# Attention, routed experts and a dense layer in one kernel: the last stage in parts of 512, 512, 512 and 256 tokens, and routing's end spread over three engines

## The chip, the cores and the metric

The kernel runs on one core of one Trainium2 chip. The metric is device time in microseconds; the median of three runs is given with the lowest and the highest. The profiles come from the hardware profiler, one execution each.

## The reference

Three steps follow one another on 4 x 448 = 1792 tokens of width 768. The kernel's output is the last step's, in float32.

```python
# attention, 4 batches, 12 heads, 448 tokens, head width 64; a sigmoid in place of a softmax
scores = q @ k.T / sqrt(64) - log(448)
x = sigmoid(scores) @ v                    # heads side by side: 1792 x 768
# experts: each token goes to one of 8, chosen by the cosine with the expert's vector
logits = normalized(x) @ normalized(expert_emb).T / tau
e = argmax(logits);  gate = softmax(logits)[e]
x = gate * (relu(x @ w1[e]) @ w2[e])       # 768 -> 1024 -> 768
# a dense layer with a rational activation, 768 -> 2048 -> 768
h = x @ w_in
P = a0 + a1*h + a2*h*h + a3*h**3;  Q = 1 + |b0|*|h| + |b1|*h*h
out = (P / (Q + 1e-6)) @ w_out
```

## The kernel before

All products that need float32 accuracy are made from a high and a low part of each operand (`fp32r`): three products on TensorE for one of the reference.

**Attention** (`attention`) runs in twelve turns `T` of two pairs of heads each, three turns a batch. A turn puts on TensorE's queue, in this order: scores, values of the turn before, scores, the transpositions of the finished heads (`transp`), the scores and values of the last 64 keys. ScalarE makes the sigmoids, VectorE copies the transposed rows out of PSUM (L241) and does side work. A batch's **routing** is a generator, `route_steps`. It is put in a queue at the end of the turn in which the batch's rows are complete; each later turn takes eight steps of it (L466), behind the turn's own instructions. Its steps on VectorE reduce the logits (L263), find the maximum and the one-hot table `OH`, copy that as bf16 to `OHb` (L282), and sum it per batch in `OHs` (L284, L287). Then come the rank products `rk` on TensorE (L295 to L305) from `OHb` and the previous batches' `OHs`, and on VectorE the rank's row and tile and the four masks `AC` (L331). The last batch is the tail: its steps are emitted without a break after the last turn and interleaved with `plan`.

**Plan** counts the tokens of each expert (`cn`, L542), makes the first tile of each expert (`bp`, copied to `bs` at L556 by VectorE), and from the masks the row list `IDX` (L580) of 21 slots of 128 rows. GpSimd gathers a slot's rows with `IDX` (L698).

**Experts** (`experts`): `x_hi` transposes a slot's rows on TensorE (L712) and casts them, `x_lo` makes the low part by two subtracting products (L718), `mm` are the expert products (L775), and the results go out by an indirect DMA on GpSimd's queue (L844). `either(s)` loads a flag on TensorE, ScalarE and GpSimd and branches between a slot with at most 64 rows in use and a full one. The first thing in a slot's `ahead` is the gather of the slot after next. VectorE turns the weights of expert after expert into high and low parts (L663, L670); before it writes a weight it waits until the last slot of the expert before has used the old one. `gates` makes the gate values, 112 tokens a line.

**The last stage** (`ffn`) goes through the tokens in `NQ` = 4 parts of 448. Each part runs over 16 blocks of 128 hidden units, 64 units in all. A unit is 18 products into `ph` (`l1`, L985 to L989), an activation of six operations on ScalarE and eight on VectorE (`act1`, `act2`), and 18 products into `acc` (`l2`, L1028 to L1030), which are emitted two units later. In the first part each block's weights are loaded, split and stored to DRAM (`load`, `split`, `keep`); the later parts fetch the split weights back (`fetch`), 2 x 768 KB a unit, two units ahead in SP's queue. The next part's rows are loaded (`rows`), gated on VectorE (`gate`, L949) and transposed on TensorE in pieces of 112 tokens (`xprep`, L958). For the first part `first_x` does that, behind 26 products of ones (L969).

Order on each engine is the order in which the instructions are written; semaphores are set by the framework.

## Time and profile before

| | |
|---|---|
| median of 3 runs | 1050.55 us (1050.28 to 1054.69) |
| the profiled execution: its time | 1050.22 us |
| its span | 1048.4 us |
| TensorE busy | 1007.6 us, 96% of the span |
| VectorE, ScalarE, GpSimd busy | 726.4, 506.0 and 136.9 us |
| granted clock of TensorE, mean | 0.987 |
| chain of waits, by engine | PE 87%, DVE 6%, DVE's queue 2%, DMA 2% |

PE is TensorE's products, PEld its weight loads, DVE is VectorE, ACT ScalarE, POOL GpSimd, SP the queue that issues most transfers. L12 is line 12 of the kernel before. Attention lasts to about 180 us, the experts to about 551 us, the last stage to the end. "Idle before" names the instruction that ended an engine's wait. In the rows the merged pieces of an engine carry a count (x12).

### The profile page before, as it was taken

What the parts mean: (1) busy time and instruction counts of PE and PEld (TensorE: products, weight loads), DVE (VectorE), ACT (ScalarE), POOL (GpSimd) and SP (SyncE); (2) the same over time, 40 slices, a digit from 0 to 9 for tenths busy, and PEclk for the clock granted to TensorE, in tenths of its full rate; (3) what the DMA queues carried; (4) which work ended last, traced back from release to release, by engine and by line L of the source; (5) the groups of instructions that cost most, each with busy time, mean ns of one, the idle gap of its engine ahead of it and who ended that gap; (6) DMA issues with size and microseconds to landing.
All of it is one profiled execution on the core that took longest, in us unless ns stands there. A gap on an engine that the chain in (4) does not pass through costs nothing.

```text
span 1048.4 us, 14336 instructions
## 1 busy us (share of the span) xinstructions
PE 1007.6 (96%) x5239; PEld 832.6 (79%) x5240; DVE 726.4 (69%) x1038; ACT 506.0 (48%) x859; POOL 136.9 (13%) x139
## 2 busy tenths in 40 slices
PE   8999998579999999999988999999999999999998
PEld 3444444468998998889876989999999999999997
DVE  1645565899607896496975999867676677666765
ACT  5556665532332323333335767655554645464453
POOL 2000000243223333243440000000000000000000
PEclk9999999699999999999998999999999999999999
DMA  7987875686906869367878996759664876548631
GB/s 216 280 229 227 256 238 182 218 269 208 360 32 206 272 204 345 104 232 272 288 261 299 381 369 269 301 189 373 208 208 151 310 290 204 205 160 327 220 128 53
DMA packets 103051, 250.19 MB, mean 239 GB/s; under 512 B 8296, under 2 KB 61928, under 8 KB 102960
## 3 DMA queue, kind: packets, MB, share of 16 engines
q1 hardware_dynamic: 99888, 234.39, 65.5%
q0 software_dynamic: 3072, 14.58, 3.9%
q8 instruction: 58, 0.95, 0.4%
q14 instruction: 33, 0.27, 0.1%
HBM read 193.88 MB, written 55.05 MB: 237 GB/s over the span
## 4 chain that ended last, share of the span: by engine, by line
PE 87%; DVE 6%; DVEq 2%; DMA 2%; issue 1%; SPq 1%; ACT 0%; POOL 0%; POOLq 0%; ACTq 0%
PE ph L775 11%; PE py L775 11%; PE ph L985 8%; PE ph L986 7%; PE acc L1028 7%; PE ph L989 7%; PE acc L1029 7%; PE acc L1030 7%; PE po L221 5%; PE sc L181 5%; DVEq L672 2%; PE po L240 2%; PE pt L712 2%; DVE w2l L670 1%; PE sc L194 1%
## 5 line engine op out<-in xcount | busy, mean ns | idle before, releaser
L985 PE MATMUL ph<-xh,wi 128*128 128x448 f32 x384 | 142.6, 371 | 0.0
L986 PE MATMUL ph<-xh,wi 128*128 128x448 f32 x384 | 140.9, 367 | 0.0
L1028 PE MATMUL acc<-gh,wo 128*128 128x448 f32 x384 | 140.5, 366 | 0.0
L1030 PE MATMUL acc<-gl,wo 128*128 128x448 f32 x384 | 140.5, 366 | 0.0
L1029 PE MATMUL acc<-gh,wo 128*128 128x448 f32 x384 | 140.5, 366 | 0.0
L994 ACT COPY h<-ph 128x448 f32<-128x448 f32 x64 | 34.0, 532 | 165.3 <-PE ph L989 164.0
L1001 DVE SCALAR_TENSOR_TENSOR sq<-sq,ab,ab 128x448 f32<-128x448 f32 x64 | 43.7, 683 | 98.4 <-ACT ab L998 98.4
L989 PE MATMUL ph<-xl,wi 128*128 128x448 f32 x384 | 88.6, 366 | 0.0
L986 PEld LDWEIGHTS ph<-xh,wi 128*128 128x128 f32 x384 | 72.6, 189 | 5.8
L985 PEld LDWEIGHTS ph<-xh,wi 128*128 128x128 f32 x384 | 72.6, 189 | 5.8
L989 PEld LDWEIGHTS ph<-xl,wi 128*128 128x128 f32 x384 | 72.1, 188 | 6.1
L1028 PEld LDWEIGHTS acc<-gh,wo 128*128 128x128 f32 x384 | 72.1, 188 | 6.1
L1030 PEld LDWEIGHTS acc<-gl,wo 128*128 128x128 f32 x384 | 72.1, 188 | 6.1
L1029 PEld LDWEIGHTS acc<-gh,wo 128*128 128x128 f32 x384 | 72.1, 188 | 6.0
L185 ACT ACTIVATE A<-sc,bias_s 128x896 f32<-128x896 f32 x72 | 67.2, 1004 | 11.2 <-PE sc L181 11.1
L663 DVE CAST w0h<-raw 128x1536 fp32r<-128x1536 f32 x14 | 12.8, 957 | 79.1 <-ACTq L788 78.2
L775 PE MATMUL py<-w2h,h 128*128 128x384 f32 x256 | 62.8, 344 | 4.3 <-DVEq L672 3.9
L775 PE MATMUL ph<-w0h,x 128*128 128x512 f32 x192 | 59.5, 410 | 7.8 <-DVEq L672 3.7
L785 ACT ACTIVATE hs<-ph 128x512 f32<-128x512 f32 x38 | 22.7, 599 | 81.5 <-PE ph L775 81.5
L775 PE MATMUL py<-w3h,h 128*128 128x384 f32 x256 | 61.3, 339 | 0.0
L181 PE MATMUL sc<-qr,kr 64*128 64x448 f32 x288 | 60.6, 553 | 0.0
L775 PE MATMUL ph<-w1h,x 128*128 128x512 f32 x192 | 60.5, 403 | 0.0
(203 smaller groups left out, 2012.0 us busy)
## 6 DMA issues: line engine op xcount, KB each, us to landing
raw<-in_w_dram SPq DMA_DIRECT2D x64, 768.0 KB
wi<-ws SPq DMA_DIRECT2D x48, 768.0 KB
wo<-ws SPq DMA_DIRECT2D x48, 768.0 KB
raw<-in_w_in_dram SPq DMA_DIRECT2D x16, 768.0 KB
raw<-in_w_out_dram SPq DMA_DIRECT2D x16, 768.0 KB
wd<-dec SPq DMA_DIRECT2D x32, 384.0 KB
rw<-wd SPq DMA_DIRECT2D x16, 768.0 KB
ws<-wi SPq DMA_DIRECT2D x16, 768.0 KB
```

What stands on the lines that cost most here:

```text
L181: nc.tensor.matmul(sc[:, r, :S], lhsT=d["k"][rs, c * P : (c + 1) * P], rhs=d["q"][rs], start=True, stop=True)
L185: nc.scalar.activation(A, sc[:, :, :S], AF.Sigmoid, bias=st["bias_s"], scale=0.125)
L221: nc.tensor.matmul(po[r * D : r * D + D, :S], lhsT=vts[pi // 3 % 2][:, c, 2 * (pi % 3) + r], rhs=d["A"][c][:, r], start=False, stop=(c == 2),)
L775: m = nc.tensor.matmul(d[u], lhsT=a, rhs=w, start=(g == 0 and n == 0), stop=(g == 1 and n == len(work) - 1))
L985: nc.tensor.matmul(ph, lhsT=w[:, 0, js], rhs=xh[:, k], start=(k == 0), stop=False)
L986: nc.tensor.matmul(ph, lhsT=w[:, 1, js], rhs=xh[:, k], start=False, stop=False)
L989: nc.tensor.matmul(ph, lhsT=w[:, 0, js], rhs=xl[:, k], start=False, stop=(k == KD - 1))
L994: nc.scalar.copy(h, ph)
L1001: nc.vector.scalar_tensor_tensor(sq, sq, ab1, ab, op0=ALU.mult, op1=ALU.add)
L1028: nc.tensor.matmul(a, lhsT=w[:, 0, js], rhs=gh, start=(f == 0), stop=False)
L1029: nc.tensor.matmul(a, lhsT=w[:, 1, js], rhs=gh, start=False, stop=False)
L1030: nc.tensor.matmul(a, lhsT=w[:, 0, js], rhs=gl, start=False, stop=(f == NF - 1))
```

## The change

- The last stage's parts are 512, 512, 512 and 256 tokens. Rows are handled in pieces of 128 tokens instead of 112. So the gate values are turned to 128 a line by two transfers through DRAM, `gd` and `gr`, on SP's queue behind the last expert's weights.
- The fetch of kept weights is written three units ahead instead of two.
- A turn of attention takes eleven routing steps instead of eight. There is one more empty step ahead of the rank products.
- In the tail the sum of the last batch's one-hot table is left out; `cn` is made by four products from `OHb` and one from the earlier sum. Two of four masks `AC` go from VectorE to GpSimd, the copy `bs` from VectorE to ScalarE. The temporaries of `plan` lie in the constants' pool.
- At the end of `plan` 16 products of ones (128 x 128 by 128 x 512, bf16) are put on TensorE; four more stand between the first slot's `x_hi` and `x_lo`, and four behind `x_lo`.
- The gather of the slot after next moves from `ahead` into the slot, behind `x_lo` of the next slot.

The diff, cut; the places left out give the activation's tiles the part's width and drop the unused pool.

```diff
--- before.py
+++ after.py
@@ -40,6 +40,8 @@
 EARLY = ((0, 0), (0, 1), (1, 0), (1, 1), (2, 0), (3, 0), (2, 1), (3, 1))
+WARM = 16
+OT = 6
 THR = 3.4332275390625e-05
...
@@ -280,13 +281,15 @@
             nc.vector.tensor_copy(ohb, oh)
-            s4 = ap.tile([P, NE], F32, name="s4")[:CP]
-            nc.vector.tensor_reduce(s4, oh.rearrange("p c e -> p e c"), axis=AX.X, op=ALU.add)
-            yield
-            if b:
-                nc.vector.tensor_add(OHs[:CP, b], s4, OHs[:CP, b - 1])
-            else:
-                nc.vector.tensor_copy(OHs[:CP, b], s4)
+            if not tail:
+                s4 = ap.tile([P, NE], F32, name="s4")[:CP]
+                nc.vector.tensor_reduce(s4, oh.rearrange("p c e -> p e c"), axis=AX.X, op=ALU.add)
+                yield
+                if b:
+                    nc.vector.tensor_add(OHs[:CP, b], s4, OHs[:CP, b - 1])
+                else:
+                    nc.vector.tensor_copy(OHs[:CP, b], s4)
+            yield
             yield
@@ -328,7 +331,7 @@
                 ci = b * NCB + c
-                nc.vector.tensor_scalar(
+                (nc.gpsimd if tail and c > 1 else nc.vector).tensor_scalar(
                     AC[:CP, ci],
@@ -463,7 +466,7 @@
                 values3(T)
-            for _ in range(8):
+            for _ in range(11):
                 if queue and next(queue[0], 1) == 1:
@@ -482,7 +485,7 @@
         norm_some(len(norms))
-        steps = plan(tc, st, pl, psc)
+        steps = plan(tc, st, cst, psc)
         for g in queue:
@@ -539,7 +542,9 @@
     cn = ps.tile([NE, 1], F32, name="cn", tag="sc")
-    nc.tensor.matmul(cn, lhsT=st["OHs"][:CP, B - 1], rhs=st["ones"][:CP, :1], start=True, stop=True)
+    for c in range(NCB):
+        nc.tensor.matmul(cn, lhsT=st["OHb"][:CP, NCH - NCB + c], rhs=st["ones"][:CP, :1], start=(c == 0), stop=False)
+    nc.tensor.matmul(cn, lhsT=st["OHs"][:CP, B - 2], rhs=st["ones"][:CP, :1], start=False, stop=True)
     yield
@@ -553,7 +558,7 @@
     bs = pl.tile([P, 2 * NE], F32, name="bs")
-    nc.vector.tensor_copy(bs, bp)
+    nc.scalar.copy(bs, bp)
     tm = pl.tile([P, NCH, NE], F32, name="tm")[:CP]
@@ -602,6 +607,9 @@
     nc.vector.tensor_copy(FL[0:1], es)
+    wp = ps.tile([P, 2, 512], F32, name="wp", tag="sc")
+    for _ in range(WARM):
+        nc.tensor.matmul(wp[:, 0], lhsT=st["ones"], rhs=st["wz"], start=True, stop=True)
 
@@ -701,6 +709,11 @@
             )
+
+        def ones(n):
+            wp = pph.tile([P, 512], F32, name="ph")
+            for _ in range(n):
+                nc.tensor.matmul(wp, lhsT=st["ones"], rhs=st["wz"], start=True, stop=True)
 
@@ -808,7 +821,6 @@
                 xg_alloc(s + 2)
-                gather(s + 2)
             if s + 1 < NSLOT:
@@ -834,6 +846,8 @@
                 x_lo(s + 1)
+            if s + 2 < NSLOT:
+                gather(s + 2)
             mm(s, 3, 0)
@@ -868,7 +882,9 @@
         x_hi(0)
+        ones(4)
         x_lo(0)
+        ones(4)
         for i in range(4):
@@ -878,6 +894,10 @@
         flush()
+        gd = drm.tile([NT], F32, name="gd")
+        st["gr"] = cst.tile([P, NT // P], F32, name="gr")
+        nc.sync.dma_start(gd.rearrange("(c p) -> p c", p=CP), st["gt"][:CP])
+        nc.sync.dma_start(st["gr"], gd.rearrange("(c p) -> p c", p=P))
         either(0)
@@ -892,10 +912,11 @@
     wd, yd, ident = st["wd"], st["yd"], st["ident"]
-    gt = st["gt"]
+    gt = st["gr"]
     co, ab1, one = st["co"], st["ab1"], st["one"]
     NF = F2 // P
-    NQ = B
+    Q = [(t, min(512, NT - t)) for t in range(0, NT, 512)]
+    NQ = len(Q)
     NU = NQ * NF
@@ -915,7 +936,7 @@
         def fetch(i):
-            if NF <= i < NU:
+            if NF <= i < NU and i not in WI:
                 pair(i)
@@ -936,50 +957,48 @@
         def rows(q, parts):
-            yq = fp.tile([P, NCB, DM], F32, name="yq", bufs=1)
-            src = yd[q * S : (q + 1) * S].rearrange("(c p) d -> p c d", p=CP)
-            n = NCB // parts
-            for c in range(0, NCB, n):
-                nc.sync.dma_start(yq[:CP, c : c + n], src[:, c : c + n])
-            X[q] = dict(y=yq)
+            t0, w = Q[q]
+            yq = fp.tile([P, 4, DM], F32, name="yq", bufs=1)
+            src = yd[t0 : t0 + w].rearrange("(c p) d -> p c d", p=P)
+            n = w // P // parts
+            for c in range(0, w // P, n):
+                nc.sync.dma_start(yq[:, c : c + n], src[:, c : c + n])
+            X[q] = dict(y=yq, n=w, c=w // P)
 
         def gate(q, c):
-            ci = q * NCB + c
-            y = X[q]["y"][:CP, c]
-            nc.vector.tensor_scalar(y, y, gt[:CP, ci : ci + 1], None, op0=ALU.mult)
+            if c >= X[q]["c"]:
+                return
+            ci = Q[q][0] // P + c
+            y = X[q]["y"][:, c]
+            nc.vector.tensor_scalar(y, y, gt[:, ci : ci + 1], None, op0=ALU.mult)
 
...
             if k == 0:
-                d["h"] = fw.tile([P, KD, S], F32R, name="xh")
-                d["l"] = fw.tile([P, KD, S], F32R, name="xl")
-            pt = pph.tile([P, 512], F32, name="ph")
-            for c in range(NCB):
-                nc.tensor.transpose(
-                    pt[:, c * CP : (c + 1) * CP], d["y"][:CP, c, k * P : (k + 1) * P], ident[:CP, :CP]
-                )
-            nc.scalar.copy(d["h"][:, k], pt[:, :S])
-            nc.vector.tensor_sub(d["l"][:, k], pt[:, :S], d["h"][:, k])
+                d["h"], d["l"] = [fw.tile([P, KD, 512], F32R, name=n)[:, :, : d["n"]] for n in ("xh", "xl")]
+            pt = pph.tile([P, 512], F32, name="ph")[:, : d["n"]]
+            for c in range(d["c"]):
+                nc.tensor.transpose(pt[:, c * P : (c + 1) * P], d["y"][:, c, k * P : (k + 1) * P], ident)
+            nc.scalar.copy(d["h"][:, k], pt)
+            nc.vector.tensor_sub(d["l"][:, k], pt, d["h"][:, k])
 
...
             d = X[0]
-            d["h"], d["l"] = [fw.tile([P, KD, S], F32R, name=n) for n in ("xh", "xl")]
+            d["h"], d["l"] = [fw.tile([P, KD, 512], F32R, name=n) for n in ("xh", "xl")]
             pts = [ppa.tile([P, 512], F32, name=f"acc{k}") for k in range(KD)]
...
                 nc.tensor.matmul(pts[0], lhsT=st["ones"], rhs=st["wz"], start=True, stop=True)
-            for c in range(NCB):
+            for c in range(4):
                 for k in range(KD):
-                    nc.tensor.transpose(
-                        pts[k][:, c * CP : (c + 1) * CP], d["y"][:CP, c, k * P : (k + 1) * P], ident[:CP, :CP]
-                    )
+                    nc.tensor.transpose(pts[k][:, c * P : (c + 1) * P], d["y"][:, c, k * P : (k + 1) * P], ident)
             for k in range(KD):
-                nc.scalar.copy(d["h"][:, k], pts[k][:, :S])
-                nc.vector.tensor_sub(d["l"][:, k], pts[k][:, :S], d["h"][:, k])
+                nc.scalar.copy(d["h"][:, k], pts[k])
+                nc.vector.tensor_sub(d["l"][:, k], pts[k], d["h"][:, k])
 
...
             xh, xl = X[i // NF]["h"], X[i // NF]["l"]
-            ph = pph.tile([P, 512], F32, name="ph")[:, :S]
+            ph = pph.tile([P, 512], F32, name="ph")[:, : X[i // NF]["n"]]
             for k in range(KD):
...
...
@@ -1019,32 +1042,33 @@
             w = WO.pop(i)
+            t0, m = Q[q]
             gh, gl = G.pop(i)
...
                     acc[o] = ppa.tile([P, 512], F32, name=f"acc{o}")
-                a = acc[o][:, :S]
+                a = acc[o][:, :m]
                 js = slice(o * P, (o + 1) * P)
...
                 if f == NF - 1:
-                    ot = fp.tile([P, S], F32, name="ot", bufs=6)
+                    ot = fp.tile([P, 512], F32, name="ot", bufs=OT)[:, :m]
                     if o % 2 and q == NQ - 1:
...
                         nc.scalar.copy(ot, a)
-                    nc.sync.dma_start(out[o * P : (o + 1) * P, q * S : (q + 1) * S], ot)
+                    nc.sync.dma_start(out[o * P : (o + 1) * P, t0 : t0 + m], ot)
 
...
         split(1)
-        rows(0, NCB)
+        rows(0, 4)
         keep(0)
...
         load(5)
-        for c in range(NCB):
+        for c in range(4):
             gate(0, c)
@@ -1053,7 +1077,7 @@
                         rows(q + 1, 1)
-                    if 5 <= f < 5 + NCB:
+                    if 5 <= f < 9:
                         gate(q + 1, f - 5)
@@ -1062,7 +1086,8 @@
                 fetch(i + 2)
-                act2(i, *act1(ph))
+                fetch(i + 3)
+                act2(i, *act1(ph, X[i // NF]["n"]))
             if i >= LF:
```

## Rows read from the trace of the kernel before

**Rows 1.** Windows by stage: busy us (instructions) of PE, PEld, DVE, ACT, POOL; clock; DMA.

```profile
20.00:180.00 160.00, 159.04 (x935) 74.76 (x935) 87.98 (x175) 95.56 (x125) 0.00 (x0) 1.00 0.79 241
...
203.00:253.00 50.00, 43.40 (x223) 37.16 (x222) 48.04 (x32) 17.08 (x38) 22.25 (x16) 0.97 0.80 262
...
565.00:685.00 120.00, 118.77 (x588) 108.41 (x587) 109.66 (x172) 81.62 (x137) 0.00 (x0) 0.99 0.88 340
```

**Rows 2.** Timeline, first and last of three batches: start us, us, engine, operation.

```profile
76.80 2.53 PE L181 MATMUL sc<-qr,kr 64*128 64x448 f32 x12
...
77.31 0.18 DVE L282 CAST OHb<-OH 112x32 bf16<-112x32 f32 x1
...
159.16 2.53 PE L181 MATMUL sc<-qr,kr 64*128 64x448 f32 x12
...
159.60 0.18 DVE L282 CAST OHb<-OH 112x32 bf16<-112x32 f32 x1
```

**Rows 3.** Timeline of routing's end for the last batch, VectorE and GpSimd.

```profile
180.68 0.60 DVE L331 TENSOR_SCALAR AC<-iof,PM,tok 112x128 f16<-112x128 f32 x2
...
185.23 1.11 DVE L331 TENSOR_SCALAR AC<-iof,PM,tok 112x128 f16<-112x128 f32 x4
...
188.50 0.18 DVE L580 TENSOR_SCALAR IDX<-ip 128x21 int32<-128x21 f32 x1 [0.25 <-PE ip L571]
...
189.55 1.11 POOL L698 DMA_INDIRECT xg<-xd,IDX  x1 [181.54 <-DVE EB L591]
```

**Rows 4.** Timeline from the gathered rows to VectorE's next weights.

```profile
193.67 1.51 PE L712 MATMUL pt<-ident,xg 128*128 128x128 f32 x6 [5.09 <-DMA xg<-xd,IDX]
...
197.99 0.77 PE L775 MATMUL ph<-w0h,x 128*128 128x512 f32 x1 [1.49 <-ACT x L719]
...
202.92 1.83 DVE L663 CAST w0h<-raw 128x1536 fp32r<-128x1536 f32 x2 [1.65 <-ACTq L788]
```

**Rows 5.** Timeline of the products of ones ahead of the last stage.

```profile
552.16 7.46 PE L969 MATMUL acc<-wz,ones 128*128 128x512 bf16 x25 [4.10 <-PEq L887]
```

**Rows 6.** Windows, the first expert products (columns as in rows 1).

```profile
198.00:201.80 3.80, 3.80 (x9) 3.03 (x10) 1.55 (x7) 2.41 (x5) 0.00 (x0) 0.50 1.03 378
```

**Rows 7.** Chain of waits, merged: start us, us, engine, tile, line, count.

```profile
257.92 6.27 PE ph L775 x27
...
270.56 6.25 PE py L775 x36
...
598.52 1.24 PE ph L989 x6
...
1024.65 1.22 PE ph L989 x6
...
1031.95 1.22 PE ph L989 x6
```

**Rows 8.** Timeline of SP's loads for the last stage and their first reader.

```profile
536.52 6.46 SPq L911 DMA_DIRECT2D rw<-wd  x3
...
551.99 0.83 ACT L930 CAST wi<-rw 128x768 fp32r<-128x768 f32 x1 [2.11 <-PEq L887]
```

**Rows 9.** Timeline of a row of products with 64 moving columns.

```profile
536.24 1.00 PE L743 MATMUL pt<-fold,hs 128*128 128x64 f32 x8
```

**Rows 10.** Waits: engine, tile, line, releaser: us in total, times, longest.

```profile
PE ph L958 <- DVE yq L949: 1.2, 1, 1.2
```

**Rows 11.** Chain of waits: the last stage's first rows.

```profile
556.42 6.18 DMA yq<-yd
```

**Rows 12.** Timeline of the last unit's activation and of the end.

```profile
1033.20 0.54 ACT L994 COPY h<-ph 128x448 f32<-128x448 f32 x1 [3.56 <-PE ph L989]
...
1039.59 0.62 DVE L1016 TENSOR_TENSOR gl<-t,gh 128x448 fp32r<-128x448 f32 x1
...
1044.14 0.62 DVE L1034 COPY ot<-acc 128x448 f32<-128x448 f32 x1 [0.59 <-PE acc L1030]
```

**Rows 13.** Windows, a stretch in which only the kept weights are fetched.

```profile
720.00:724.00 4.00, 4.00 (x21) 3.71 (x20) 2.40 (x5) 2.71 (x5) 0.00 (x0) 1.00 1.02 419
```

20 lines of the change are left out of this document (11 added, 9 removed).

## The prediction

> **What bounds the kernel now.** I read three views, in this order. First the busy time by stage [rows 1]: in attention TensorE is busy for 159.04 of 160 us, so any wait put in front of it there is paid in full. From 203 to 253 us it is VectorE that is full (48.04 of 50 us): it splits the weights of the first experts, and the experts' products wait for it. In the first part of the last stage TensorE is full again (118.77 of 120 us) with VectorE close behind (109.66). Second the timeline of the three places where TensorE stands still: between attention and experts, where the chain of routing, the gather and the first products follow one another; between experts and last stage; and after the last product. Third the chain of waits and the waits by name, for the price of a product and for what stops TensorE in the last stage. Their rows are named where they are used.
>
> The sum is made against the profiled execution, 1050.22 us with a span of 1048.4 us; it lies 0.3 us under the median of the three runs, 1050.55 us.
>
> **Eleven routing steps instead of eight.** A batch's routing is a generator of which TensorE's rank products are one step. With eight steps in a turn the rank products fall into the next turn, when VectorE's one-hot table is long done. With eleven they are the eleventh step of the same turn and stand in TensorE's queue right behind the values products, ahead of the next scores. TensorE reaches that place at 76.80 us, but the table in bf16 (L282) ends only at 77.31 + 0.18 = 77.49 us [rows 2]; with 0.05 us for the signal that is a wait of 0.74 us. Behind the waiting product all scores and values are queued, and TensorE has no slack here [rows 1]. There are three such batches, each with the same order; the last one gives 159.60 + 0.18 + 0.05 - 159.16 = 0.67 us [rows 2]. Sum 3 x 0.7 = **+2.1 us**; bounds 0 (TensorE late for another reason) and 2.4.
>
> **The chain of routing for the last batch.** The eleven steps take leftovers of batch 2, 0.60 us, out of the way (first row of [rows 3]). Two of four masks go to GpSimd: 0.56 of 1.11 us on VectorE (second row of [rows 3]). The count from four products of bf16 tables and one sum costs TensorE four products more and VectorE a reduction and an addition less; I take it at nothing. The copy of the bases on ScalarE saves VectorE one short copy; it goes into the margin, because GpSimd's two masks beside VectorE may cost as much. So the indices come 1.2 us earlier, at 188.50 - 1.2 = 187.3 us. From indices to first transposition the trace has 193.67 - 188.50 = 5.2 us [rows 3, 4], most of it the gather; its data would be there at 192.5 us.
>
> **The products of ones** are queued on TensorE between routing's last product (about 187.2 us) and the transpositions of the first rows. Their price is bounded from both sides: 25 of the same shape took 7.46 us, partly at half clock [rows 5], so 16 take 4.8 us at that pace; at half clock throughout nine products of 512 columns took 3.80 us [rows 6], so 16 take 6.8 us. I take 5.9 us: they end at 193.1 us (192.0 to 194.0), after the data, and eat most of what the shorter chain gains. The transpositions then start at 193.1 instead of 193.67 us. From there to the first expert product the trace has 197.99 - 193.67 = 4.3 us [rows 4]: transpositions, a cast, two subtracting products, and then some two microseconds in which TensorE's sequencer loads the slot's flags and branches. At full clock the first items are shorter, but two times four ones (0.86 us each at full clock) are queued among them, and the second four stand ahead of the flag's load. Net I take +0.6 us (0 to 0.9), so the first product starts at 198.0 us, as before. What is gained is the clock: the clock granted from 198.0 to 201.8 us was 0.50, the 1.2 GHz level [rows 6], and the slot's first twelve products ran until VectorE went on at 202.92 us [rows 4]. At full clock twelve cost 12 x 0.232 = 2.8 us [rows 7], so VectorE can go on at 201.0 us: **-1.9 us** (bounds -2.5, where VectorE's own gates are next, and +0.5, if the clock is low again). This counts in full, since VectorE is the bound up to 253 us.
>
> The transpositions of the first rows ran at the low clock and did not raise it [rows 4, 6]. The Trainium skill (TensorE: Matmul & The Clock Gate, section on PE-mode transpose) says that a transposition doesn't count as activity for the clock; by that rule the ones have to carry it alone, and the gap while the sequencer branches speaks against them. That is a rival below.
>
> **Moved transfers.** The gather of the rows after next moves from ahead of a slot to its middle, on GpSimd's queue behind the slot's subtractions. It needed 4.1 us to its use [rows 3, 4]; it has a slot's products left, over 27 x 0.232 + 36 x 0.174 = 12.5 us [rows 7]. Nothing, and GpSimd's subtractions come earlier, under VectorE's bound. The two transfers that turn the gate values from 112 to 128 lines go on SP's queue behind the last expert weights, ahead of the last stage's loads, and the second waits for the first to land. Behind them stand loads that were issued by 543 us and read first at 551.99 us [rows 8]. Elements of 4 bytes have no row here; as long as both together stay under 9 us they cost nothing, so I take 0 (0 to 2).
>
> **The last stage.** Its columns are the same, 3 x 512 + 256 = 4 x 448, and so are its 2304 products. The price follows the columns: 384 columns 6.25 / 36 = 0.1736 us, 448 columns 7.30 / 36 = 0.2028 us, 512 columns 6.27 / 27 = 0.2322 us [rows 7]; per column that is 0.452, 0.453, 0.4535 ns. At 0.4525 ns 256 columns cost 0.116 us. A floor by the weights' load shows where 64 moving columns still took (1.00 - 0.22) / 7 = 0.111 us from start to start, the last one's 0.22 us taken as its length [rows 9], under 0.116. Before: 2304 x 0.2028 = 467.3 us, and about 1 us more since the first part ran at 1.24 / 6 = 0.2067 us for its first seven units. After: 1728 x 0.2322 + 576 x 0.116 = 468.1 us. Taken at **-0.6 us**; bounds: 512 columns at the lower price per column and 256 at the floor give -4, 256 columns at 0.123 us and the first part slower in the same proportion give +6.
> TensorE's one pause, 1.2 us before a transposition that waited for VectorE's gating [rows 10], goes: a unit of 36 products lasts 8.36 us instead of 7.44 and VectorE's operations on 512 columns grow by about half a microsecond. **-1.2 us** (0 to -1.2). 72 transpositions of 112 columns become 60 of 128, 5% fewer columns: nothing. The first rows are 128 lines a transfer instead of 112, 14% more of the 6.18 us that they are waited for [rows 11]: **+0.5 us** (0 to 0.9).
> At the end the last unit's activation runs from 1033.20 to 1040.21 us while TensorE does two blocks of second products [rows 12]; it just fitted. With 256 columns the two blocks last 36 x 0.116 = 4.2 us. Scaled by columns the activation would take 4.0 us, unscaled 7.0; half of it fixed gives 5.4: a new wait of 1.2 us. The last copy (0.62 us, [rows 12]) and the stores shrink by some 0.4 us. **+0.8 us** (-0.4 to +2.4).
> A unit of the last part fetches 1.573 MB in 4.2 us, 375 GB/s; the same fetch ran at 419 GB/s [rows 13], so it keeps up. The Trainium skill (DMA: Bandwidth & Descriptors, Specifications) gives about 358 GB/s per core, by which the part would be short by 0.2 us a unit; the trace disagrees, and the measurement decides. Even at the 340 GB/s of the mixed stretch [rows 1] it would miss 16 x 0.43 = 7 us, less than the three units (12.6 us) by which the buffers lead.
>
> **Sum:** 2.1 - 1.9 - 0.6 - 1.2 + 0.5 + 0.8 = -0.3 us, so 1050.22 - 0.3 = **1049.9 us**.
>
> **Rivals.** (a) The gains come and the waits don't: routing's wait is covered (0 instead of +2.1), the products take their lower prices (-3.5), the end fits (0). Sum -1.9 - 3.5 - 1.2 + 0.5 = -6.1: 1044 us. For it: the price per column of the shorter products is the lower one. Against it: the order of the queue in [rows 2] leaves no cover. (b) Slower: a product of 256 columns doesn't get below the time that loading and handing over its weights takes. Each nanosecond over 0.116 us costs 576 x 0.001 = 0.58 us; from 0.127 us on the whole is over 0.5% slower, at 0.13 us it is 1058 us. For it: a weights record lasts about 0.19 us, more than the product. Against it: [rows 9]. (c) The change doesn't do what it says: the clock is low again at the first product, so the ones only delay; +0.5 instead of -1.9 gives 1052 us. (d) The last part waits for its fetches: only below 315 GB/s (16 x 0.79 us a unit use up the lead); at 290 GB/s 16 x 1.2 - 12.6 = 7 us more, 1057 us. Against it: [rows 13].
>
> **How the numbers follow.** Forecast 0.60, (a) 0.20, (b) 0.09, (c) 0.09, (d) 0.02. A measurement of this kernel can tell about 0.5%, 5.3 us, from no change. Case (a) is faster and the forecast reaches under 1045.3 us in a few cases; (b) and a rest of the forecast are slower: faster 0.22, same 0.66, slower 0.12. The forecast alone spans 1046 to 1054 us; the range takes in most of (a) and (c) and a part of (b): 1044.0 to 1055.5 us.
>
> **What would show it.** A wait of 0.7 us on TensorE before the rank products in three turns of attention; ones ending between 192 and 194 us plus that shift, with transpositions right behind; granted clock 1.00 at the first expert products; 0.232 and 0.116 us a product in the last stage; no pause before the transpositions; a wait of about 1.2 us before the last block. It is wrong above all if 256 columns cost more than 0.12 us, or if the rank products don't wait.

## The result

The changed kernel takes 1044.81 us (median of 8 runs, 1041.90 to 1047.02) against 1051.87 us of the kernel before on the same chip (8 runs, 1047.35 to 1054.69): ratio 0.9911, 95% interval 0.9881 to 0.9940. It is faster by 0.9%. No change was forecast as likeliest, at 1049.9 us; the time lies inside the range, near its lower end. The profiled execution of after took 1043.8 us with a span of 1042.0 us, 6.4 us under the 1048.4 us of before.

Cut into stretches at events that both traces have (end of the last product of attention, VectorE's last weights of its full stretch, at 253.3 and 254.7 us, end of the experts' products, first and last product of the last stage, end), the spans divide so, in us:

| stretch | before | after | difference |
|---|---|---|---|
| start to end of attention | 180.28 | 184.32 | +4.04 |
| to VectorE's last weights | 73.01 | 70.37 | -2.64 |
| to the end of the experts' products | 294.77 | 294.62 | -0.15 |
| hand-over, to the first product of the last stage | 17.16 | 18.95 | +1.79 |
| first to last product of the last stage | 478.52 | 469.27 | -9.25 |
| to the end | 4.67 | 4.50 | -0.17 |

The gain is in the last stage, where I had put -1.8 us. Everything else together costs 2.9 us. Of the 4.04 us in attention 2.2 us are the waits ahead of the rank products; the other 1.9 us lie ahead of 40 us, in a pause and half clock behind it that come with the execution and not with the change (both below).

The windows of after, with the columns of [rows 1]: attention is 2 us less busy than before, VectorE is full as before, and from 201.1 us the first expert products have the full clock that [rows 6] lacked.

```profile
20.00:180.00 160.00, 157.04 (x912) 73.02 (x910) 87.34 (x175) 95.12 (x124) 0.00 (x0) 0.98 0.80 242
205.00:255.00 50.00, 44.24 (x222) 38.16 (x221) 47.77 (x33) 16.63 (x37) 25.24 (x15) 0.93 0.78 259
568.00:688.00 120.00, 119.87 (x541) 98.57 (x539) 111.88 (x162) 83.53 (x130) 0.00 (x0) 1.00 0.84 324
...
201.10:204.00 2.90, 2.90 (x13) 2.35 (x14) 1.12 (x5) 2.40 (x5) 0.00 (x0) 1.00 1.03 381
```

The timeline of after, first of three batches: the rank products stand where [rows 2] had the next scores, and wait for VectorE. By the row it was the sum `s` (L286), right behind the bf16 table, that ended the wait. The other two waits are 0.61 us each (from 120.69 and 162.58 us on).

```profile
79.17 0.18 DVE L283 CAST OHb<-OH 112x32 bf16<-112x32 f32 x1
79.26 0.20 DVE L286 TENSOR_REDUCE s<-OH 112x8 f32<-112x32 f32 x1
...
79.49 0.19 PE L298 MATMUL rk<-OHb,low 112*112 112x32 bf16 x1 [0.77 <-DVE s L286]
```

The timeline of after from routing's end to VectorE's next weights (answers [rows 3, 4]): the masks are shared, the transpositions follow the ones without a gap, the first product comes 16.75 us behind attention instead of 17.71, and VectorE's weights 20.81 us behind it instead of 22.64.

```profile
188.66 0.66 DVE L334 TENSOR_SCALAR AC<-iof,PM,tok 112x128 f16<-112x128 f32 x2
188.73 1.67 POOL L334 TENSOR_SCALAR AC<-iof,PM,tok 112x128 f16<-112x128 f32 x2 [180.56 <-DVE PM L329]
...
191.29 0.18 DVE L585 TENSOR_SCALAR IDX<-ip 128x21 int32<-128x21 f32 x1 [0.24 <-PE ip L576]
...
191.30 6.08 PE L612 MATMUL wp<-wz,ones 128*128 128x512 bf16 x16
...
192.34 1.10 POOL L706 DMA_INDIRECT xg<-xd,IDX  x1 [1.94 <-issue]
...
197.21 0.82 PE L725 MATMUL pt<-ident,xg 128*128 128x128 f32 x6
...
201.07 0.48 PE L788 MATMUL ph<-w0h,x 128*128 128x512 f32 x1 [0.62 <-PE ph L716]
...
205.13 0.96 DVE L671 CAST w0h<-raw 128x1536 fp32r<-128x1536 f32 x1 [0.78 <-DVE gt L632]
```

The chain of waits of after, merged, six second-half products of a unit with 512 and with 256 columns (answers [rows 7]): 1.36 / 6 = 0.2267 us and 0.72 / 6 = 0.120 us.

```profile
579.63 1.36 PE ph L1008 x6
...
1021.07 0.72 PE ph L1008 x6
```

The timeline of after at the hand-over: the store of the gate values goes out at 531.99 us, the load that waits for its landing only at 543.14 us, and four loads of the last stage follow in a burst (before had its four from 531.49 to 542.98 us; [rows 8] shows the last three). TensorE stands still for 8.71 us ahead of its ones, where [rows 5] had 4.10. Behind the ones it is the other way round: before waited twice for the gated rows, 2.0 us in all (its waits, first row; the lines after it are the timeline of after), and after starts its transpositions at 565.34 us without a wait. From the start of the ones to the first product it took 13.06 us before and 10.24 us after. So the hand-over's +1.8 us are 4.6 us more of pause less 2.8 us behind it.

```profile
PE acc L972 <- DVE yq L949: 2.0, 2, 1.7
```

```profile
531.99 0.50 SPq L899 DMA_DIRECT2D gd<-gt  x1
...
543.14 0.37 SPq L900 DMA_DIRECT2D gr<-gd  x1
543.60 2.84 SPq L932 DMA_DIRECT2D rw<-wd  x4
...
558.02 7.48 PE L990 MATMUL acc<-wz,ones 128*128 128x512 bf16 x26 [8.71 <-PEq L907]
565.34 2.78 PE L993 MATMUL acc<-ident,yq 128*128 128x128 f32 x24
```

The end of after (answers [rows 12]): from the last unit's first copy to its products 4.63 us, and a wait of 0.35 us.

```profile
1030.47 0.37 ACT L1016 COPY h<-ph 128x256 f32<-128x256 f32 x1 [1.58 <-PE ph L1008]
...
1035.10 0.39 PE L1052 MATMUL acc<-gh,wo 128*128 128x256 f32 x1 [0.35 <-DVE gh L1038]
```

### The profile page after: what moved, and what is told of

It reads as the page before. It is cut to its first block, busy times and chain, and to the rows that moved or that the text cites. A ratio compares the mean times of both kernels' runs of the same rounds, so it can differ in the third digit from the quotient of the medians.

```text
span 1042.0 us, 14389 instructions
## 1 busy us (share of the span) xinstructions
PE 1006.0 (97%) x5256; PEld 794.5 (76%) x5256; DVE 722.6 (69%) x1031; ACT 507.1 (49%) x860; POOL 143.6 (14%) x141
## 5 line engine op out<-in xcount | busy, mean ns | idle before, releaser
L1052 PE MATMUL acc<-gh,wo 128*128 128x512 f32 (+1 forms) x384 | 139.3, 363 | 0.3 <-DVE gh L1038 0.3
L1054 PE MATMUL acc<-gl,wo 128*128 128x512 f32 (+1 forms) x384 | 139.4, 363 | 0.0
L1053 PE MATMUL acc<-gh,wo 128*128 128x512 f32 (+1 forms) x384 | 139.2, 363 | 0.0
L1004 PE MATMUL ph<-xh,wi 128*128 128x512 f32 (+1 forms) x384 | 137.8, 368 | 0.1
L1005 PE MATMUL ph<-xh,wi 128*128 128x512 f32 (+1 forms) x384 | 136.1, 363 | 0.0
L1016 ACT COPY h<-ph 128x512 f32<-128x512 f32 (+1 forms) x64 | 34.1, 533 | 158.0 <-PE ph L1008 158.0
L1023 DVE SCALAR_TENSOR_TENSOR sq<-sq,ab,ab 128x512 f32<-128x512 f32 (+1 forms) x64 | 43.8, 684 | 90.6 <-ACT ab L1020 90.5
L1008 PE MATMUL ph<-xl,wi 128*128 128x512 f32 (+1 forms) x384 | 87.2, 363 | 0.0
L1053 PEld LDWEIGHTS acc<-gh,wo 128*128 128x128 f32 x384 | 72.5, 189 | 11.1
L1008 PEld LDWEIGHTS ph<-xl,wi 128*128 128x128 f32 x384 | 66.7, 189 | 11.2
L242 DVE COPY xr<-po 112x272 f32<-112x272 f32 x48 | 21.1, 442 | 62.0 <-PE po L241 61.5
```

Of the source, the lines that this page charges most:

```text
L1004: nc.tensor.matmul(ph, lhsT=w[:, 0, js], rhs=xh[:, k], start=(k == 0), stop=False)
L1005: nc.tensor.matmul(ph, lhsT=w[:, 1, js], rhs=xh[:, k], start=False, stop=False)
L1008: nc.tensor.matmul(ph, lhsT=w[:, 0, js], rhs=xl[:, k], start=False, stop=(k == KD - 1))
L1016: nc.scalar.copy(h, ph)
L1023: nc.vector.scalar_tensor_tensor(sq, sq, ab1, ab, op0=ALU.mult, op1=ALU.add)
L1052: nc.tensor.matmul(a, lhsT=w[:, 0, js], rhs=gh, start=(f == 0), stop=False)
```

## The experiments

Each group ran with runs of the kernel before on the same chip; a ratio is to those. Single traces differ at a place that no kernel here changes: a pause of TensorE of 1.1 to 3.0 us at about 14 us, in all traces but one put down to a load of the queries, with the clock at 0.50 after it in some executions. Attention then ends up to 4 us later, so stretches are compared, not spans.

### Which part of the change gains

The last stage alone: the kernel before, with the last stage, its gate transfers and its fetches from after.

```diff
-        NQ = B
+        Q = [(t, min(512, NT - t)) for t in range(0, NT, 512)]
+        NQ = len(Q)
```

> The kernel before with the last stage's changes alone (parts of 512, 512, 512 and 256 tokens, the two transfers of the gate values, fetches three ahead); routing, ones and gather are as before. Theory P (price per product: 448 columns cost 2.7 to 6.7 ns more than the line N/2.4 + 13.3 ns on which 384, 512 and 256 lie): first product to last product of the last stage falls from 478.5 to about 469.3 us, the hand-over from experts to last stage grows from 17.15 to about 19 us; together 7 to 7.5 us faster than before, ratio 0.993. Rival R (the gain came from routing, the ones or the clock ahead of the experts): within 1.5 us of before, ratio 0.999 to 1.001, and products at 0.2028 x 512/448 = 0.232 us.

1041.70 us against 1055.35 us, ratio 0.9877 [0.9853, 0.9901]. First to last product 469.25 us, hand-over 18.39 us. This is the whole gain of the change and more; R falls. It is also more than the 7 to 7.5 us that P had worked out from one trace of before: the kernel before was slower beside this run, and the next group shows what can make it so.

The rest alone: after with the last stage of before.

```diff
-        Q = [(t, min(512, NT - t)) for t in range(0, NT, 512)]
-        NQ = len(Q)
+        NQ = B
```

> The kernel after with the last stage of before (four parts of 448, gates read directly): eleven steps, spread chain, ones and gather move alone. Theory P: rank products wait 3 x 0.67 = +2.0 us, the tail and the first products at full clock give -1.8 us, so +0.2 us: ratio 0.999 to 1.002, and a hand-over of about 17 us as before, since the two transfers of gate values are not there. Rival R: 4 us or more faster, ratio under 0.996. Rival H (the longer hand-over comes from the moved gather or the longer program, not from the gate values): hand-over about 19 us here too, ratio about 1.002 to 1.003.

1050.30 us, ratio 0.9969 [0.9947, 0.9991]: a little faster, more than P said and less than R. Its waits ahead of the rank products are 0.77, 0.61 and 0.61 us, its hand-over 16.32 us (H falls), and VectorE's last weights come 70.71 us behind attention (before 73.01). Its 448-column products took 202.7 to 202.8 ns in this trace, the low end of what follows, so part of its lead may be that. One pause of before shows in it too, 2.30 us at 628.57 us.

### The price of a product

The kernel before, operands 512 elements apart, still 448 columns.

```diff
-                d["h"] = fw.tile([P, KD, S], F32R, name="xh")
+                d["h"] = fw.tile([P, KD, 512], F32R, name="xh")[:, :, :S]
...
-            gh = fp.tile([P, S], F32R, name="gh", bufs=3)
+            gh = fp.tile([P, 512], F32R, name="gh", bufs=3)[:, :S]
```

> The kernel before with one change: the operands of the last stage's products (the high and low halves of rows and activations) lie 512 elements apart instead of 448; the products still take 448 columns and the work is the same. Theory S (the extra 2.7 to 6.7 ns a product come from where the rows of the moving operand begin, at multiples of 1792 bytes): products at 200.0 us/1000, 2304 x 2.7 to 6.7 ns = 7 to 8 us less, ratio about 0.993. Theory N (they come from the number of columns, 448, itself): products at 202.7 to 206.7 ns as before, ratio 1.000.

1055.55 us, ratio 0.9995 [0.9974, 1.0015], products at 203.9 to 206.7 ns by part: N holds. But the parts had other paces than in the trace of before (205.1, 203.4, 203.4, 202.7 ns there). Two more executions of before show whether that is chance.

> The kernel before, looked at once more. Theory P (the pace of 448-column products is fixed anew in each part of each execution, between 202.7 and 206.8 ns, and this spreads the kernel's times): from first to last product of the last stage 475 to 485 us and not the same as in the other looks, and the execution's time follows it. Rival (the spread comes from the start and the hand-over alone): 478.5 us within 0.3 us, as in the first profile.

> The kernel before, looked at a third time. Theory P: again a last stage of 475 to 485 us that differs from the other looks. Rival: 478.5 us within 0.3 us.

Their times are 1051.37 and 1058.72 us, first to last product 481.15 and 485.58 us against 478.52 in the first trace; the products of the four parts took 205.1, 203.4, 203.6, 206.7 and 203.8, 205.9, 205.9, 206.7 ns. P holds. The chain of waits of the second of them, the same six products in its third and fourth parts; in [rows 7] the last two units took 1.22:

```profile
852.29 1.24 PE ph L989 x6
...
1032.79 1.24 PE ph L989 x6
```

By contrast nine traces with 512 and 256 columns lie between 469.22 and 469.27 us from first to last product. So the mean pace of 448-column products moves between 202.7 and 206.7 ns, from part to part and from one execution to the next. Over 2304 products that is up to 9 us. From the first trace of before to the slowest the last stage grows by 7.1 us of the 8.5 us by which the times differ, so this can be most of the spread of before's times (1047 to 1060 us over all groups).

Taken 18 products at a time, all five traces with 448 columns show two paces and not a spread: 202.4 to 202.9 and 206.6 to 206.7 ns a product. In six units of each part but the last, the next part's rows are transposed among the products, and only there does the pace change. From the last transposition of one part through the first half of the next it holds, and so it does all through the last part. What chooses the pace isn't known.

Other counts of columns, in one run:

```diff
+    V = [480, 320, 416, 192]
...
-            ph = pph.tile([P, 512], F32, name="ph")[:, : X[i // NF]["n"]]
+            ph = pph.tile([P, 512], F32, name="ph")[:, :v]
```

> The changed kernel whose last stage multiplies only 480, 320, 416 and 192 columns in its four parts, instead of 512, 512, 512 and 256 (the other columns are left out, and their outputs are copies of others): the price of a product by its column count, in one run. Theory L (only an odd multiple of 64 leaves the line N/2.4 + 13.3 ns, as 448 does): 480 takes 213.3 and 416 186.7 ns, on the line; 320 takes 149 to 153 ns instead of 146.7 and 192 takes 96 to 100 instead of 93.3. Theory F (448 alone is odd, or wide products alone): 320 at 146.7 and 192 at 93.3 ns. Rival (b) of the forecast (a floor by the weights' load): 192 columns stay above 105 ns.

970.96 us, with less to multiply: the kernel leaves the other columns out. Its chain of waits, six products in each part:

```profile
663.21 1.30 PE ph L1010 x6
...
728.75 0.88 PE ph L1010 x6
...
817.08 1.13 PE ph L1010 x6
...
906.47 0.67 PE ph L1010 x6
```

320 columns take 0.88 / 6 = 146.7 ns, on the line, so L falls: an odd multiple of 64 can lie on it. 480 take 217 ns, 3.4 above it, and 416 take 186.7 to 188.3 ns (1.12 or 1.13 us for six), on it or 1.7 above, again two paces that change at the transpositions. So 448 isn't alone, and it isn't the wide ones either, since 512 is on the line: F falls too. 192 take 112 ns instead of 93.3: there is a floor as in rival (b), below 256 columns, at the 111 ns that 64 columns took in [rows 9]. Fetches don't set it: that part has one wait for them, of 0.32 us. The rows give 256, 320, 384 and 512 columns at N/2.4 + 13.3 ns; what sets 448 and 480 apart stays open. That the fetches run three units ahead isn't the gain: in the last stage of before the trace has no wait of TensorE but the one of [rows 10].

### Eleven steps

```diff
-            for _ in range(11):
+            for _ in range(10):
```

> The kernel after with ten routing steps in a turn instead of eleven, so that the rank products are the first step of the next turn. If the three waits of 0.77, 0.61 and 0.61 us are paid in full: no wait ahead of the rank products, attention ends 2.0 us earlier, and 2.0 us faster than after (VectorE's stretch behind it starts 2.0 us earlier). Rival: VectorE has the same work in attention and is late at its end by as much, the waits move to another place: under 0.5 us faster than after.

1042.11 us, ratio 0.9876 [0.9851, 0.9902] (after had 0.9911 and 0.9907 beside other runs of before). No wait stands ahead of the rank products. The traces of all runs show the price: from the 81st score product (at 36 to 41 us, behind the pause at the start) to the end of attention it is 142.7 us in each of the twelve with eight or ten steps and 144.8 to 145.0 us in each of the eight with eleven. So the waits are paid in full in attention, 2.2 us. In this run's trace the lead was given back at the experts' end: behind a pause of 2.15 us at 542.6 us the clock fell, and TensorE took its last 12 products at half pace. Its windows, columns as in [rows 1]:

```profile
542.50:545.60 3.10, 0.95 (x6) 0.87 (x6) 2.07 (x2) 0.00 (x0) 1.24 (x1) 1.00 0.57 50
545.70:549.10 3.40, 3.40 (x12) 3.24 (x11) 0.00 (x0) 0.95 (x2) 0.98 (x1) 0.50 0.97 280
```

The same step once more stands between two kernels below: with ten steps 1042.86, with eleven 1046.62 us on one chip, though the intervals of their ratios overlap.

### The products of ones

The changed kernel again as a measure, then without any ones, then without the two groups of four.

> The changed kernel once more, word for word, as the measure for the runs beside it. Its last stage has no product of 448 columns. Theory P: first to last product of the last stage again 469.3 us, while a run of before takes 475 to 484 us by the pace its 448-column products fall into; the changed kernel's times lie closer together than those of before, about 5 us against 10 us. Ratio to before 0.987 to 0.993.

1046.40 us, ratio 0.9907 [0.9886, 0.9928]; last stage 469.25 us, hand-over 20.51 us.

```diff
-WARM = 16
+WARM = 0
...
-        ones(4)
         x_lo(0)
-        ones(4)
```

> The changed kernel without any of the products of ones around the first gather (16 and twice 4). If they bring the clock: granted clock 0.50 at the first expert products, twelve of them 4.5 to 4.9 us instead of 2.8, but transpositions start when the gather lands, about 1.2 us after it did before, so VectorE goes on 0.5 to 1.5 us later than in after: 0.5 to 1.5 us slower. Rival (the clock rises by itself, the ones only delay): first product 1 to 2 us earlier at full clock and 1 to 2 us faster than after.

1046.83 us, ratio 0.9900 [0.9877, 0.9922]. The clock is 0.50 at the first products (from 200.6 to 204.5 us nine of them, as in [rows 6]), and VectorE's weights start 22.02 us behind attention instead of 20.81. But at the end of VectorE's stretch only 0.2 to 0.5 us of these 1.2 us are left (70.82 us behind attention against 70.37 and 70.65 in the two traces of after), and the time doesn't tell the kernels apart. Between its first and last weights VectorE runs the same 32 operations in both, 46.84 us of work without the ones and 47.59 us in after; why they are shorter isn't shown.

> The changed kernel with the 16 products of ones ahead of the transpositions, but without the two groups of four among them. If the sixteen alone hold the clock up to the first products: granted clock 1.00 there and the first product about 1.5 us earlier, 1 to 1.7 us faster than after. If the transpositions and the branch let it fall again: clock 0.50 at the first products, and 0 to 1 us slower than after.

1046.15 us, ratio 0.9887 [0.9856, 0.9918]. Clock 1.00 at the first products, which come 16.83 us behind attention: neither of the two cases. The sixteen alone hold the clock across the transpositions and a pause of 1.60 us, and the fours cost nothing, because they stood in that pause.

### The hand-over

The store and the load of the gate values at other places among the weight loads:

```diff
+            if e == 1:
+                nc.sync.dma_start(gd.rearrange("(c p) -> p c", p=CP), st["gt"][:CP])
+            if e == 3:
+                nc.sync.dma_start(st["gr"], gd.rearrange("(c p) -> p c", p=P))
```

> The changed kernel with the store of the gate values issued behind expert 1's weight loads and the load behind expert 3's, instead of both in a row behind expert 7's. Theory G (the store's 11 us of small elements on the queue ahead of the last stage's loads bunch these loads at the end of the experts, and that slows the branch and the rows): loads spread from 531 us on as in before, pause of TensorE ahead of the ones 4 to 5.5 us instead of 8.7, hand-over 17 us instead of 18.95: 1.5 to 2 us faster than after. Rival B (the pause comes from the longer program or the later last slot): pause 7.8 to 8.7 us, time as after within 0.5 us.

1044.29 us, ratio 0.9870 [0.9841, 0.9900]; hand-over 17.78 us against 20.51 us beside it, pause ahead of the ones 5.77 us. G holds, but the store now delays weights that VectorE waits for: its last weights come 72.21 us behind attention instead of 70.65.

With 4 and 6 in place of 1 and 3:

> The changed kernel with the store of the gate values behind expert 4's weight loads and their load behind expert 6's, where TensorE and not VectorE's weights set the pace. Theory G: TensorE's pause ahead of the ones 4 to 6 us and a hand-over of about 17.5 us as with the store behind expert 1, but without what that store cost in VectorE's stretch up to 253 us (a wait of 5.2 instead of 2.2 us at 234 us): 2 to 3 us faster than the changed kernel, ratio to it 0.997 to 0.998. Rival B: time as the changed kernel within 0.5 us.

1046.62 us, ratio 0.9927 [0.9899, 0.9956]: nothing gained that shows beside the 0.9907 and 0.9911 of the changed kernel, so G isn't borne out. The loads are spread again, but the pause is 7.76 us, and a gather comes late behind the store (timeline, TensorE):

```profile
385.15 0.85 PE L725 MATMUL pt<-ident,xg 128*128 128x128 f32 x6 [2.69 <-DMA xg<-xd,IDX]
```

What the pause consists of shows in the instructions of its line: two branches out of the experts' last, skipped slots, on TensorE's sequencer. Before, then after (min/median/max ns):

```profile
L887 PEldq COMPARE_BRANCH  x7: 67/68/3306, 461.3 to 549.1; - x7
```

```profile
L907 PEldq COMPARE_BRANCH  x7: 68/68/5522, 463.3 to 552.6; - x7
```

The two long ones took 3.31 and 2.76 us before, 5.52 and 5.12 after. In each the trace has one packet of 16384 bytes on the instruction queue. Before it began 1.00 and 0.33 us behind the branch's start, after 3.17 and 2.76 us; in all four the branch ended 2.3 to 2.4 us behind the packet's start, and in both branches of all twenty traces 2.3 to 2.7 us. What lies ahead of it is data: the transfers from 545 to 552.5 us before and from 546 to 558 us after (packets, MB, share of the engines).

```profile
q1 hardware_dynamic: 106, 0.55, 17.8%
q8 instruction: 2, 0.03, 1.7%
```

```profile
q1 hardware_dynamic: 566, 3.08, 64.2%
q0 software_dynamic: 128, 0.59, 17.3%
q8 instruction: 2, 0.03, 1.0%
```

The second branch took 4.0 to 5.4 us in the seven traces with the late 4-byte store, and 2.7 to 3.1 us in the other thirteen. The first took 5.5 to 7.4 us with the store, 3.3 to 3.8 us in before and its like, 3.9 to 6.6 us in the rest: the store isn't all of it. That the code waits behind data was read from these packets, not tried by itself.

### Versions that take the costs back

Ten steps, and the gate values behind experts 4 and 6:

> The two costs taken back together: ten routing steps in a turn (no wait ahead of the rank products, 2.0 us) and the gate values moved behind experts 4 and 6 (2 to 3 us). If both are paid in full: 4 to 5 us faster than the changed kernel, about 0.986 to 0.988 of before on a chip where the changed kernel stands at 0.991. If the clock's falls behind short pauses eat them: 2 us faster.

1042.86 us, ratio 0.9912 [0.9887, 0.9937], 3.8 us under the kernel with eleven steps beside it. The ratio is that of the changed kernel and not the 0.986 to 0.988 of both costs paid back. In its trace the pause is 5.46 us, with the transfers where they went with 7.76 us above.

The same with other parts:

```diff
-    Q = [(t, min(512, NT - t)) for t in range(0, NT, 512)]
+    Q = [(0, 512), (512, 512), (1024, 384), (1408, 384)]
```

> The kernel of the two costs taken back, with parts of 512, 512, 384 and 384 tokens instead of 512, 512, 512 and 256. 384 columns at 173.3 ns lie on the same line: 1152 x 0.2267 + 1152 x 0.1733 = 460.8 us, as with 512 and 256; the wait of 0.35 us ahead of the last block goes, the last copies and stores grow by about 0.3 us: the same within 0.5 us. If the price of 384 columns here were like that of 448 (2.7 to 6.7 ns above the line), 3 to 8 us slower.

1038.94 us, ratio 0.9868 [0.9829, 0.9907]: products at 173.3 ns, last stage 468.43 instead of 469.22 us, no wait at the end. With the shorter end that is 0.9 us; the other 3 us between the medians aren't explained by it (attention ended 4 us earlier in this trace, by the pause at the start).

The gate values turned on TensorE, so that whole lines are stored and loaded (with ten steps and the parts of 384):

```diff
+        nc.tensor.transpose(pt[:NCH, 0, :CP], st["gt"][:CP], ident[:CP, :CP])
+        nc.scalar.copy(gT, pt[:NCH, 0, :CP])
+        nc.sync.dma_start(gd.rearrange("(c p) -> c p", p=CP), gT)
+        nc.sync.dma_start(st["g2"], gd.rearrange("(c p) -> c p", p=P))
```

> The changed kernel with ten routing steps a turn, parts of 512, 512, 384 and 384, and the gate values turned by two small transpositions on TensorE, so that both transfers move whole lines (16 of 448 bytes out, 14 of 512 bytes in) and no element of 4 bytes goes through a queue. Theory G (the 11 us of the small elements bunch the last stage's loads behind them): store and load land within 2 to 3 us each, loads issued from 532 to 543 us as in before, hand-over 15.5 to 17.7 us, no stall of a gather at 380 us; 4 to 6 us faster than the changed kernel, 1038 to 1041 us. Rival B (the hand-over is long for another reason): hand-over 19 us, 2 to 3 us faster than the changed kernel.

> The same with the gather of the rows after next issued ahead of a slot again, as in before. If the moved gather is what lengthens TensorE's pause ahead of the slot at 430 us (1.3 to 1.5 us in the kernels with the gather ahead, 1.9 to 2.7 in the others, mostly with 3.4 us at half clock behind it): pause 1.3 to 1.5 us, no fall of the clock there, 0.6 to 2.2 us faster than with the gather in the middle. If it is the longer program: pause 1.9 us or more, time the same within 0.5 us.

1037.68 us, ratio 0.9844 [0.9808, 0.9879], and with the gather ahead 1039.63 us, 0.9857 [0.9821, 0.9893]. The store of lines lands sooner than that of elements, but behind the weights in its queue it still took 6.0 us instead of the 2 to 3 that G had, and the hand-over is 17.39 us (17.2 to 18.3 us in the four traces of this pair and the next). Against the kernel before this one, on another chip, the intervals overlap, so what turning the values brings isn't shown. The moved gather does lengthen the pause at 430 us; timelines of the first and of the second kernel:

```profile
430.19 0.47 PE L788 MATMUL ph<-w0h,x 128*128 128x512 f32 x1 [1.97 <-issue]
```

```profile
429.31 0.47 PE L788 MATMUL ph<-w0h,x 128*128 128x512 f32 x1 [0.97 <-ACT ys L817]
```

Whether it costs time the pair told a second time:

> The kernel with turned gate values once more, word for word, as the measure for the run beside it. From VectorE's last weights of its full stretch to the experts' end 295.5 to 298 us, a pause of 1.9 us or more ahead of the slot at 430 us. If the moved gather's price shows in the time: 1 to 2 us slower than the run beside it.

> The kernel with turned gate values and the gather ahead of a slot, once more, word for word. From VectorE's last weights of its full stretch to the experts' end 294.2 to 295.1 us, as in all kernels with the gather ahead, 1.8 us less than the mean of the others. If that is paid in full: 1 to 2 us faster than the run beside it; if the hand-over gives it back: the same within 0.5 us.

1037.81 us, ratio 0.9843 [0.9813, 0.9873], and 1038.03 us, 0.9840 [0.9808, 0.9872]: the same. From VectorE's last weights to the experts' end the first took 294.76 us, not the 295.5 to 298 expected, and the second 294.20 us; in the first pair it was 296.21 and 294.46 us. No half clock followed the pause in either trace with the gather in the middle (it followed in the trace of the rest alone, from 432.1 to 435.4 us); the slower one had another pause of 1.1 us at 520 us. These kernels are faster than both: 0.9843 of before, where the change reached 0.9907 and 0.9911.

## Why the prediction was wrong

**The last stage's products: the step that failed.** "The price follows the columns" at 0.4525 ns per column was taken at -0.6 us (its own terms, 468.1 against 467.3 + 1, give -0.2). From the measured prices, 1728 x 0.2267 + 576 x 0.120 = 460.8 us, against 469.2 us for the products in the trace of before (its four paces times 576): -8.4 us. The pause that went and 0.4 us more for the rest make it the -9.25 us of the table. The 512-column price had been taken from the experts, whose products run at 0.2322 us on other operands, and 448 was read as one more point of a line through the origin. [rows 7] held the warning: six products of 448 columns took 1.24 us at 598.52 and 1.22 us at 1024.65, so their price wasn't a matter of columns alone, and 2304 x 0.0033 = 7.7 us hung on it. I used that pair as "about 1 us more", not as a sign against the law. One column a cycle at the 2.4 GHz level, with the fixed rest from the 384 columns of [rows 7] (0.1736 - 0.160 = 0.0136 us), would have given 0.2269 and 0.1203 us, 461.4 us in all, and 0.2003 us for 448, under both of its rows. Seen afterwards that is a sign that 448 is the dear one, though the experts' 512 columns lie 5 ns above that line too, on their own operands. That the time still fell inside the range is luck, since costs that the sum didn't have took a part of the gain back: 1.8 us at the hand-over and, in the trace, 1.9 us at the start.

**The gate transfers: also failed.** "As long as both together stay under 9 us they cost nothing": the store alone took 11.1 us, and the cost didn't arise where I looked, at the loads' first reader, but at TensorE's branches: its pause grew by 4.6 us, and the hand-over, with the rows no longer late, by 1.8 us here and by 3.4 us in the second trace of after. With the last stage alone changed it is 18.39 us, with the rest alone 16.32 us, so the longer one comes with the last stage's part of the change. How much of it the store makes isn't settled: with the store behind expert 4 the pause was 7.76 and 5.46 us. The Trainium skill (DMA: Bandwidth & Descriptors, Specifications) asks for transfers of at least 512 bytes for full rate; with 1792 elements of 4 bytes the trace agrees, 11.1 us for 7 KB; lines of 448 bytes in the same place took 6.0 us, so about half of it goes by the size of the pieces. The Trainium skill also gives a compare-and-branch 108 ns (Advanced Engine Details and Errata, Control Flow Timing): the median of the seven on this line is 68 ns, but the two with a packet of code in them took 2.7 to 7.4 us.

**Eleven steps: right.** 0.77 + 0.61 + 0.61 = 2.0 us, 2.2 us by the end of attention, against +2.1.

**Routing's end and the ones: right in sum, wrong in shares.** VectorE's weights start 1.8 us earlier (forecast -1.9), and its stretch ends 2.6 us earlier. The clock rose as foreseen; transpositions alone left it at 0.50 [rows 6], and again in the kernel without ones. The rule of the Trainium skill (TensorE: Matmul & The Clock Gate, section on PE-mode transpose) that a transposition doesn't count for the clock agrees with both. But the kernel without ones has 2.2 of the 2.6 us by the end of VectorE's stretch (70.82 against 73.01), so the ones bring 0.2 to 0.5 us in the end and the rest of the change the most; I had put it the other way round. What takes the ones' gain back are longer operations of VectorE, 47.59 us of them against 46.84; what makes them longer wasn't separated.

**Moved gather: nothing in the time, but not nothing in the traces.** In both pairs it lengthens a pause by 1.0 us and shortens VectorE's stretch from its first to its last weights by 0.5 us (49.6 against 50.1). From there to the experts' end the thirteen traces with it took 294.6 to 297.9 us, the seven without it 294.2 to 295.1. The times of the pairs don't show that, and the trace of after has 294.62, so the forecast of nothing fits it by chance.

**Pause and first rows.** The pause of 1.2 us is gone; in three other traces with 448 columns it was 2.3 us. The rows weren't late: the pause ahead of the ones was longer, and the transpositions follow the ones without a gap. So from the ones to the first product it is -2.8 us instead of +0.5, out of the time that the longer pause had cost.

**The end: mis-sized.** The activation took 4.63 us, two thirds of its 7.0 us; by these two about 1.5 us of it are fixed, an estimate, and the prediction had half of it fixed; the wait was 0.35 us instead of 1.2, and the end came 0.2 us sooner instead of 0.8 later.

**Rivals.** (a) gave 1044 us, nearly the result, and by luck: it looked for the gain in the products, but at -3.5 us and by a price per column, and its condition was wrong, for the rank products do wait. Its doubt about the price deserved more than 0.20. (b) has its floor at 112 ns, under the 120 ns that 256 columns take. (c) the clock was full. (d) the last part fetched at 420 and 382 GB/s (windows from 980 and 1000 us) with TensorE busy throughout.

## What to carry to other kernels

Price a product from the same shape, operands and stage, and when two rows give one shape two prices, treat the difference as the largest open term of the sum and not as noise. A width whose products run at an unsteady pace costs its mean and spreads the times; one on the steady line can be had for the same work by cutting the parts differently. A small transfer in a queue is to be priced by what stands behind it, down to the packets of code in an engine's branches.

## What the hardware showed

- Products of the last stage at full clock: 120.0, 173.3 and 226.7 ns for 256, 384 and 512 columns in every trace that has them; in one trace 146.7 ns for 320, 186.7 to 188.3 for 416, 217 for 480 and 112 for 192. 448 columns take 202.6 or 206.7 ns, and change from one to the other only where transpositions stand among them.
- Two branches of TensorE held a packet of 16384 bytes on the instruction queue and ended 2.3 to 2.7 us behind its start, in every trace. They took 2.7 us where the DMA engines stood idle and up to 7.4 us in a burst of data; that the packet waits behind the data is read from this, not tried.
- At 430 us TensorE paused for 1.9 to 2.7 us in the thirteen traces with the moved gather. In six of them the granted clock was 0.50 for 3.4 us behind it, in seven it stayed at 1.00; in the seven traces with pauses of 0.9 to 1.5 us there it stayed.
